# Sink scores and sink AV of a streaming attention as 32-wide tiles of TensorE, with AV banks by head pair

## The chip, the cores and the metric

The kernel runs on one core of a Trainium2 chip. A core has five engines with instruction queues of their own: TensorE (PE in the profile, its weight loads PEld), VectorE (DVE), ScalarE (ACT), GpSimd (POOL) and SyncE (SP). They meet through semaphores. TensorE writes into PSUM, which has eight banks here, and the other engines take the results from there into SBUF. The metric is device time in microseconds (us), the median of several executions.

## What is computed

Sliding-window attention with a few "sink" keys that every query sees, followed by a feed-forward network with the maximum of three products:

```python
batch, n_heads, seq, head_dim = (4, 8, 768, 64)
n_sink, window = (4, 128)
scores = scale * (q @ k.T)
is_sink = pos[None, :] < n_sink
rel = pos[:, None] - pos[None, :]
keep = is_sink | ((rel >= 0) & (rel < window))
a = softmax(where(keep, scores, -1e9))
attn = a @ v                             # heads side by side: x is 3072 x 512
h = maximum(maximum(x @ w1, x @ w2), x @ w3)     # 512 -> 768
out = h @ w_out                          # 768 -> 512
```

Inputs and output are float32; the kernel computes in bfloat16 with float32 sums.

## The kernel before

The 3072 tokens are cut into 12 chunks of 256 queries, three for each of the four batches (`CPB` is 3). A chunk's eight heads are four pairs, one head on partitions 0 to 63, the other on 64 to 127. Chunk number `ci` belongs to batch `ci // 3`; where `ci % 3` is 0 the sink keys lie in the chunk's own window blocks and no separate sink step is needed. The other eight chunks need one.

The order of the work is written out by hand, as strings of short tokens. A token is a step, a letter for a chunk relative to the loop, and an argument. `K`/`Q` transpose keys or queries on TensorE (chunks 0 to 3), `D` has the DMA do it (later chunks) and `E` places the result; `B` and `S` are window scores and their exponentials, `M` the mask, `Z` the sink scores, `X` the copies of sink keys, `A` the product with v, `T` the transpose of x, `F0` to `F8` the nine groups of the first feed-forward layer (number n uses weight n % 3), `Y` and `W` the output layer, `L` the loads. Each engine takes its instructions in this order.

- **Sink keys** (`sink_k`, L235 to L242): for a new batch, four small copies put the four sink keys of each head into a zeroed 128-column stationary matrix `ks` for each pair. For batch 0 ScalarE makes them, for the others VectorE.
- **Sink scores** (`sink_score`, L286 to L296): four matmuls, one per pair, each 128 x 128 stationary and 256 columns, add up into one bank. Row 8x + head of the result is sink key x of that head. One exponential gives `e_sink`.
- **Sink v** (`sink_v`, L171 to L176): the 32 rows of sink v are multiplied by a mask `bm` on GpSimd, so that a row is zero outside its own head's 64 columns, and its last column, where the softmax's sum comes from, is one only there. The result `vs` has 8 x 65 columns for each batch; all of it is zeroed first by ScalarE (L117).
- **AV** (`av`, L300 to L321): a call handles four heads (`g`) and one half of the queries (`t`). In a chunk with sinks it starts with one matmul of `e_sink` against 260 columns of `vs` (L304), then adds eight matmuls of 65 columns (L312). VectorE takes a reciprocal of the sums (L317) and multiplies (L320) into `x_sb`. The calls go in the order g0 t0, g0 t1, g1 t0, g1 t1 in the loop.
- **Transposes of x** (`xpose`, L325): by TensorE and a copy up to chunk 4, later by the DMA from SP's queue. The transpose of half t needs the two calls of `av` that write this half.

All PSUM tiles come from one pool of eight banks with one tag. A tile gets the bank that was given out eight tiles earlier, and its first writer waits until that bank's readers are done.

In the loop over `i`, the letters a, b, c, d, e stand for chunks i to i+4. So TensorE works on the feed-forward of chunk i, on AV of chunk i+1 and the scores of chunk i+2 in one iteration. Before the loop stands a hand-made start in which weights and first chunks arrive. There the loads of weights are issued on GpSimd's queue, among its casts, and some loads are held back by a one-element write of an engine (`load(2, nc.scalar)`): that engine's place in its own queue decides when the load begins.

Of the kernel before, what the change touches and what calls it, by code (L numbers as in the profile page):

```python
# [16 lines left out]
def kernel(  # L17
# [33 lines left out]
    with tc.manual_schedule():  # L51
# [50 lines left out]
        kk = [const.tile([128, NP, 256], BF16, name=f"kk{i}") for i in range(2 * CPB)]  # L102
        qT = [const.tile([128, 2, NP, 128], BF16, name=f"qT{i}") for i in range(2 * CPB)]
        ve = [const.tile([128, S // 128, H, D + 1], BF16, name=f"ve{i}") for i in range(2)]
        ks = [const.tile([128, NP * 130], BF16, name=f"ks{i}") for i in range(2)]
        vs = const.tile([128, B, H, D + 1], BF16, name="vs")

        ident = const.tile([128, 128], BF16, name="ident")
        make_identity(nc, ident)
# [4 lines left out]
            for _ in range(n):  # L114
                nc.tensor.matmul(wp, lhsT=ident, rhs=ident, start=True, stop=True)  # L115

        nc.scalar.copy(vs.rearrange("p b h d -> p (b h d)"), zc.to_broadcast([128, B * H * (D + 1)]))  # L117
        nc.vector.memset(ve[0][:, :, :, D:D + 1], 1.0)
        nc.vector.memset(ks[0], 0.0)

# [39 lines left out]
                    in_=moe_w_out[384 * a:384 * a + 384].rearrange("(a p) f -> p a f", p=128))  # L160


        bm = const.tile([R, H], F32, name="bm")

        def sink_v_init():
            nc.gpsimd.memset(bm, 0.0)
            for x in range(n_sink):
                nc.gpsimd.affine_select(out=bm, in_=bm, compare_op=ALU.not_equal, fill=1.0,
                                        base=-H * x, pattern=[[-1, H]], channel_multiplier=1)

        def sink_v(b):  # L171
            nc.gpsimd.tensor_tensor(
                out=vs[0:R, b, :, 0:D],
                in0=vs_raw[:, b].unsqueeze(1).to_broadcast([R, H, D]),
                in1=bm.unsqueeze(2).to_broadcast([R, H, D]), op=ALU.mult)
            nc.gpsimd.tensor_copy(vs[0:R, b, :, D:D + 1], bm.unsqueeze(2))  # L176

        bfs = {}

# [52 lines left out]
                    out=dst.rearrange("p i a t -> p (i a) t"),  # L232
                    in_=bfs[ci][:, j].rearrange("p i a x -> p (i a x)"))

        def sink_k(b, copy=nc.vector.tensor_copy):  # L235
            kv = ks[b % 2].rearrange("p (a y) -> p a y", y=130)[:, :, 0:8 * n_sink]
            for h in range(2):
                hp = slice(64 * h, 64 * h + 64)
                for i in range(2):
                    copy(  # L240
                        kv[hp].rearrange("p a (t i x) -> p i a t x", i=2, x=8)[:, i, :, :, h],
                        kk[b * CPB % (2 * CPB)][hp, :, 64 * i:64 * i + n_sink // 2])  # L242

        es = {}
# [41 lines left out]
        def sink_score(ci):  # L286
            b, c = divmod(ci, CPB)
            st = psum.tile([128, 256], F32, tag="f", name="sk")
            for p in range(NP):
                nc.tensor.matmul(st, lhsT=ks[b % 2][:, p * 128:(p + 1) * 128],  # L290
                                 rhs=qT[ci % (2 * CPB)][:, :, p].rearrange(
                                     "p i (n t) -> p n i t", n=2),
                                 start=(p == 0), stop=(p == NP - 1))
            e = work.tile([128, 256], BF16, tag="e_sink", bufs=2, name="e_sink")
            nc.scalar.activation(e, st, AF.Exp, scale=scale)  # L295
            es[ci, "sink"] = e  # L296

        xs = {}

        def av(ci, g, t):  # L300
            b, c = divmod(ci, CPB)
            o = psum.tile([128, 4, D + 1], F32, tag="f", name="o_ps")
            if c > 0:
                nc.tensor.matmul(o, lhsT=es[ci, "sink"][:, t * 128:(t + 1) * 128],  # L304
                                 rhs=vs[:, b, 4 * g:4 * g + 4, :], start=True, stop=False,
                                 skip_group_check=True)
            for hh in range(4):
                p, h = divmod(4 * g + hh, 2)
                blocks = [(sl, n) for sl, n in ((2 * t, 2 * c + t - 1), (2 * t + 1, 2 * c + t))
                          if n >= 0]  # L310
                for x, (sl, n) in enumerate(blocks):
                    nc.tensor.matmul(o[:, hh], lhsT=es[ci, p][:, h, sl],  # L312
                                     rhs=ve[b % 2][:, n, 2 * p + h],
                                     start=(c == 0 and x == 0), stop=(x == len(blocks) - 1),
                                     skip_group_check=True)
            rc = work.tile([128, 4], F32, tag="rc", bufs=4, name="rc")
            nc.vector.reciprocal(rc, o[:, :, D])  # L317
            if g == 0:
                xs[ci, t] = work.tile([128, H, D], BF16, tag="x", bufs=4, name="x_sb")
            nc.vector.tensor_mul(xs[ci, t][:, 4 * g:4 * g + 4], o[:, :, 0:D],  # L320
                                 rc.unsqueeze(2).to_broadcast([128, 4, D]))  # L321

        xTs = {}

        def xpose(ci, t):  # L325
            if t == 0:
                xTs[ci] = work.tile([128, 2, DS, 128], BF16, tag="xT", bufs=3, name="xT")
            if ci > CPB + 1:
                nc.sync.dma_start_transpose(
                    out=xTs[ci][:, t], in_=xs.pop((ci, t)).rearrange("p h d -> p (h d)"))  # L330
                return
            pt = psum.tile([128, DS, 128], BF16, tag="f", name="xt_ps")
            x = xs.pop((ci, t)).rearrange("p h d -> p (h d)")
            for ds in range(DS):
                nc.tensor.transpose(pt[:, ds], x[:, ds * 128:(ds + 1) * 128], ident)  # L335
            copy = nc.vector.tensor_copy if ci == 0 else nc.scalar.copy
            copy(xTs[ci][:, t], pt)  # L337
# [57 lines left out]
        def step(op):  # L395
# [6 lines left out]
            elif name == "D":  # L402
                turn(ci)
            elif name == "L":
                load(ci)
            elif name == "E":
                place_k(ci, kTs.pop(ci), slice(0, NP))
            elif name == "S":
                score(ci, [int(x) for x in arg])
            elif name == "B":  # L410
                score_banks(ci, [int(x) for x in arg])
            elif name == "M":
                mask(ci, [int(x) for x in arg])
            elif name == "Z":
                if ci % CPB:
                    sink_score(ci)
            elif name == "X":
                if ci % CPB == 0:
                    sink_k(ci // CPB)
            elif name == "A":  # L420
                av(ci, int(arg[0]), int(arg[1]))
            elif name == "T":
                xpose(ci, int(arg))
            elif name == "F":
                ffn_h(ci, int(arg))
            elif name == "Y":
                ffn_y(ci, [int(arg)], [range(FB)])
            elif name == "W" and ci == NCH - 1:
                ffn_y(ci, [0], [range(FB)])
                ffn_y_end(ci)  # L430
            elif name == "W":
                ffn_y(ci, [0, 1], [range(4), range(4, FB)])

        def run(text, **at):
# [23 lines left out]
        cast_qk(1, 0, 0, nc.vector)  # L458
        cast_qk(1, 1, 0, nc.vector)
        cast_v(0, 1, None, (0,))  # L460
        sink_k(0, nc.scalar.copy)
        cast_qk(1, 0, 1, nc.gpsimd)
        cast_qk(1, 1, 1, nc.gpsimd)
        load_w(1, 0, 256)
        sink_v(0)
        load_w(1, 256, d_ff)
        load_w(2)
        cast_v(1, 0, nc.gpsimd, (0,))
        warm(3)
        run("Aa00 Aa10 Kb0 Qb0", a=0, b=1)  # L470
        run("Aa01 Aa11 Bb01", a=0, b=1)
        run("Sb01 Kb1 Qb1 Ta0 Ta1 Bb23", a=0, b=1)
        run("Sb23 Zb Fa0", a=0, b=1)
        cast_v(1, 0, nc.vector, (1,))
        cast_v(1, 1, nc.vector, (1,))
        cast_v(1, 1, None, (0,))
        run("Fa3 Ab00 Ab10 Ab01 Ab11 Fa6 Tb0 Tb1 Fa1", a=0, b=1)
        load(2, nc.scalar)
        cast_qk(2, 0, 0, nc.gpsimd)
        cast_qk(2, 1, 0, nc.gpsimd)  # L480
        load_wo()
# [2 lines left out]
        load(3, nc.gpsimd)  # L484
        cast_v(2, 0, nc.gpsimd)
        cast_v(2, 1, nc.gpsimd)
        run("Fb0 Fb3 Fb6 Fb1 Fa4 Fa7 Fb4 Fb7 Kc0 Qc0 Fa2 Kc1 Qc1 Fa5 Sc01 Mc01 Fa8 Zc Fb2",
            a=0, b=1, c=2)
        nc.gpsimd.memset(ks[1], 0.0)
        nc.gpsimd.memset(ve[1][:, :, :, D:D + 1], 1.0)  # L490
        cast(3)
        for b in range(1, B):
            sink_v(b)
        load(4)
        run("Fb5 Sc23 Mc23 Ac00 Fb8 Ac01 Ya0 Ya1", a=0, b=1, c=2)
        cast(4)
        run("Ac10 Ac11 Yb0 Tc0 Tc1 Kd0 Qd0 Yb1 Kd1 Qd1", b=1, c=2, d=3)
        run("Zd Sd0123 Md0123 De Lf", d=3, e=4, f=5)

        for i in range(2, NCH):  # L500
# [1 line left out]
                cast(i + 3)  # L502
            text = "Fa0 Fa1 {} Fa2 {} Zc Sc0123 Mc0123 Wa0"
            if i == 2:
                text = text.format("", "Ab00 Fa3 Ab01 Xb Fa4 Ab10 Fa5 Ab11 Fa6 Dd Le Fa7 Fa8 Ya0 Ec Tb0 Tb1 Ya1")
                text = text.replace(" Wa0", "")
            elif i == CPB:
                text = text.format("Ec", "Fa3 Ab00 Fa4 Ab01 Fa5 Ab10 Fa6 Ab11 Dd Le Fa7 Fa8 Tb0 Tb1")
            elif i < 0:
                text = text.format("Ec", "Ab00 Fa3 Xb Ab01 Fa4 Ab10 Fa5 Ab11 Fa6 Dd Le Fa7 Tb0 Tb1 Fa8")  # L510
            else:
                text = text.format("Ec", "Ab00 Fa3 Xb Ab01 Fa4 Ab10 Fa5 Ab11 Tb0 Tb1 Fa6 Dd Le Fa7 Fa8")
            run(text, a=i, b=i + 1, c=i + 2, d=i + 3, e=i + 4)

        for pool in (psum, work, raw, const):
# [36 lines left out]
```

## Time and profile before

| | |
|---|---|
| median of 5 runs | 185.48 us (184.14 to 186.94) |
| the profiled execution | 185.48 us |
| its span in the profile | 183.8 us |
| TensorE busy, matmuls | 172.8 us (94%) |
| TensorE weight loads | 136.6 us (74%) |
| VectorE busy | 119.6 us (65%) |
| ScalarE busy | 91.7 us (50%) |
| GpSimd busy | 71.1 us (39%) |
| granted TensorE clock | 0.994 |

The span runs from the first to the last instruction in the trace; the device time has a little around it. "Busy" of TensorE counts each matmul from start to modelled end, and neighbouring matmuls overlap in a pipeline, so a matmul's own duration is much longer than the step from one to the next. The chain that ended last is followed backwards from the last instruction; in it, a group of matmuls stands with the time by which it moved the end. A group of instructions has the form "line, engine, operation, output<-input, shape, count | busy us, mean ns of one | idle time just before, and what ended it". In a timeline the two leading numbers are start and length in us.

### The profile page before, as it was taken

Reading aid. Unit: us, or ns where it says so; the run is one execution under the profiler, and the core shown is the slowest. Engines: PE = TensorE matmul, PEld = TensorE weight load, DVE = VectorE, ACT = ScalarE, POOL = GpSimd, SP = SyncE. Lnnn points to the kernel's source line nnn. Section 1 sums busy time; section 2 is a strip of 40 time slices with the busy share of each in tenths; the row PEclk is TensorE's granted clock in tenths of the full one; section 3 lists DMA queues with packets and bytes.
Section 4 is the critical chain, followed back from the end, with each engine's and each line's share of the span. In section 5 each row is a group of like instructions: output and inputs, shape, how many; then the busy total and the mean of one; then the engine's idle time right before and its main releaser. Section 6 shows DMA issues by size and latency. Waiting matters only on the chain.

```text
span 183.8 us, 4636 instructions
## 1 busy us (share of the span) xinstructions
PE 172.8 (94%) x1836; PEld 136.6 (74%) x1849; DVE 119.6 (65%) x257; ACT 91.7 (50%) x186; POOL 71.1 (39%) x122
## 2 busy tenths in 40 slices
PE   6987999999997899999999999999999999999990
PEld 6744889876685589589598698697796796896870
DVE  2594626787499189577669686686596775672450
ACT  6398461654941781961832923914716626622210
POOL 7394107748993665392044227145054000000000
PEclk9999999999999999999999999999999999999997
DMA  4999989999878989893698799895996742131404
GB/s 143 296 213 242 213 191 262 208 285 295 253 166 257 203 242 262 229 248 82 145 254 235 158 299 218 224 292 138 146 360 144 92 103 44 43 103 29 116 0 114
DMA packets 68022, 34.67 MB, mean 189 GB/s; under 512 B 26145, under 2 KB 64801, under 8 KB 68001
## 3 DMA queue, kind: packets, MB, share of 16 engines
q1 hardware_dynamic: 64784, 30.45, 65.3%
q0 software_dynamic: 3056, 3.67, 11.4%
q8 instruction: 14, 0.23, 0.5%
q10 hardware_dynamic: 160, 0.26, 0.4%
q14 instruction: 8, 0.06, 0.1%
HBM read 25.20 MB, written 6.29 MB: 171 GB/s over the span
## 4 chain that ended last, share of the span: by engine, by line
PE 79%; DMA 8%; DVE 4%; ACT 2%; issue 1%; POOL 1%; SPq 1%; ACTq 0%; DVEq 0%
PE h_ps L350 48%; PE y_ps L370 16%; DMA v_raw<-in_v_dram 8%; PE o_ps L312 5%; PE st L271 4%; DVE h_sb L356 3%; PE o_ps L304 2%; PE sk L290 2%; SPq L70 1%; POOL ve L197 1%; PE xt_ps L335 1%; PE pt L218 1%; ACT xT L337 1%; DVE x_sb L320 1%; POOL w L150 0%
## 5 line engine op out<-in xcount | busy, mean ns | idle before, releaser
L350 PE MATMUL h_ps<-xT,w 128*128 128x256 bf16 x864 | 103.1, 273 | 1.3 <-DMA w<-in_moe_w_dram 1.2
L350 PEld LDWEIGHTS <-w 128*128 128x128 bf16 x864 | 81.5, 98 | 12.7 <-DMA w<-in_moe_w_dram 1.5
L356 DVE TENSOR_TENSOR h_sb<-h_sb,h_ps 128x512 bf16<-128x512 bf16 x72 | 49.1, 684 | 25.9 <-PE h_ps L350 20.5
L277 ACT ACTIVATE e_sb<-st 128x512 bf16<-128x512 f32 (+1 forms) x96 | 45.1, 591 | 6.9 <-PE st L271 6.9
L188 POOL CAST qk_bf<-qk_raw 128x512 bf16<-128x512 f32 x42 | 28.8, 698 | 50.7 <-DMA qk_raw<-in_k_dram 38.0
L354 ACT CAST h_sb<-h_ps 128x512 bf16<-128x512 f32 x36 | 21.8, 611 | 49.5 <-PE h_ps L350 49.5
L284 DVE TENSOR_TENSOR e_sb<-e_sb,msk 128x1024 bf16<-128x1024 bf16 (+1 forms) x40 | 29.3, 739 | 19.1 <-ACT e_sb L277 19.0
L370 PE MATMUL y_ps<-wo,h_sb 128*128 128x512 bf16 x126 | 31.7, 379 | 2.3 <-DVE h_sb L356 1.6
L197 POOL CAST ve<-v_raw 64x512 bf16<-64x512 f32 x42 | 26.8, 638 | 17.0 <-DMA v_raw<-in_v_dram 13.5
L370 PEld LDWEIGHTS <-h_sb 128*128 128x128 bf16 x138 | 12.8, 98 | 16.2 <-DVE h_sb L356 2.8
L320 DVE TENSOR_TENSOR x_sb<-o_ps,rc 128x256 bf16<-128x256 f32 x48 | 20.4, 424 | 1.6
L312 PE MATMUL o_ps<-ve,e_sb 128*128 128x65 bf16 x352 | 19.0, 193 | 0.9 <-ACT e_sb L277 0.5
L312 PEld LDWEIGHTS <-e_sb 128*128 128x128 bf16 x352 | 17.0, 98 | 2.7 <-ACT e_sb L277 1.1
L380 ACT COPY y_sb<-y_ps 128x512 f32<-128x512 f32 x22 | 12.6, 633 | 11.0 <-PE y_ps L370 10.9
L271 PE MATMUL st<-qT,kk 64*128 64x128 bf16 (+1 forms) x256 | 13.2, 237 | 0.5 <-ACT qT L221 0.3
L271 PEld LDWEIGHTS <-kk 64*128 64x128 bf16 x256 | 8.8, 94 | 5.0 <-issue 3.8
L304 PE MATMUL o_ps<-vs,e_sink 128*128 128x260 bf16 x32 | 8.8, 274 | 0.0
L317 DVE RECIPROCAL rc<-o_ps 128x4 f32<-128x4 f32 x48 | 8.4, 175 | 0.4 <-PE o_ps L312 0.2
L221 ACT COPY qT<-pt 128x512 bf16<-128x512 bf16 x6 | 3.6, 592 | 7.7 <-PE pt L218 7.7
L115 PE MATMUL warm<-ident 128*128 128x128 bf16 x43 | 5.0, 307 | 1.4 <-POOL ident masks.py:199 1.4
L295 ACT ACTIVATE e_sink<-sk 128x256 bf16<-128x256 f32 x8 | 3.2, 394 | 6.4 <-PE sk L290 6.4
L208 DVE COPY kk<-pt 128x512 bf16<-128x512 bf16 x8 | 3.4, 421 | 4.1 <-PE pt L218 4.1
(52 smaller groups left out, 82.5 us busy)
## 6 DMA issues: line engine op xcount, KB each, us to landing
qk_raw<-in_k_dram SPq DMA_DIRECT2D x24, 256.0 KB, 4.1
qk_raw<-in_q_dram SPq DMA_DIRECT2D x24, 256.0 KB, 3.6
v_raw<-in_v_dram SPq DMA_DIRECT2D x11, 512.0 KB, 5.9
out_dram<-y_sb SPq DMA_DIRECT2D x22, 256.0 KB, 4.4
w<-in_moe_w_dram POOLq DMA_DIRECT2D x2, 768.0 KB, 10.8
wo<-in_moe_w_out_dram POOLq DMA_DIRECT2D x2, 384.0 KB, 7.3
v_raw<-in_v_dram POOLq DMA_DIRECT2D x1, 512.0 KB, 9.8
w<-in_moe_w_dram POOLq DMA_DIRECT2D x1, 512.0 KB, 9.3
```

Of the source, the lines that this page charges most:

```text
L188: (eng.tensor_copy if eng else nc.scalar.copy)(dst.rearrange("p i (h d) -> p h i d", d=D), src)
L197: (eng.tensor_copy if eng else nc.scalar.copy)(dst[64 * i:64 * i + 64], src[64 * n:64 * n + 64, :, i])
L271: nc.tensor.matmul(st[h][:, sl], lhsT=kx[r, p, k0:k0 + 128], rhs=qx[r], start=ci >= 2, stop=True, skip_group_check=ci < 2)
L277: nc.scalar.activation(e[:, h, lo:], st[:, lo:], AF.Exp, scale=scale)
L284: nc.vector.tensor_tensor(out=e, in0=e, in1=m, op=ALU.mult)
L312: nc.tensor.matmul(o[:, hh], lhsT=es[ci, p][:, h, sl], rhs=ve[b % 2][:, n, 2 * p + h], start=(c == 0 and x == 0), stop=(x == len(blocks) - 1),
L320: nc.vector.tensor_mul(xs[ci, t][:, 4 * g:4 * g + 4], o[:, :, 0:D], rc.unsqueeze(2).to_broadcast([128, 4, D]))
L350: nc.tensor.matmul(hp[:, f], lhsT=w_sb[wi, 2 * fp + f][:, ds], rhs=xTs[ci][:, :, ds], start=(ds == 0), stop=(ds == DS - 1))
L354: nc.scalar.copy(dst, hp)
L356: nc.vector.tensor_max(dst, dst, hp)
L370: nc.tensor.matmul(yps[ci, t], lhsT=hs[ci][:, fb, t * 128:(t + 1) * 128], rhs=wo[:, fb], start=(fb == 0), stop=(fb == FB - 1))
L380: nc.scalar.copy(y[:, t], yps.pop((ci, t)))
```

## The change

Both sink products become four independent tiles of the array.

- **Sink scores**: a pair's sink keys take a 32-column stationary matrix (8 columns used), and its result goes to 32 partitions of its own, 32p and on, of the one bank. Each matmul is a sum of its own. Row 32p + 2x + h is sink key x of head h in pair p.
- **Sink v**: a selection matrix `sel` is made on GpSimd from the identity. Two matmuls, one for each h, spread the 32 rows of sink v with a column of ones to those partitions for all four batches at once; VectorE copies them to `vs`. ScalarE casts the 32 rows first (into `v_sink`). The mask, its products on GpSimd (one per batch) and the zeroing of `vs` by ScalarE go.
- **Sink AV** is a step of its own, `V`, ahead of the chunk's first `A`. It takes four banks, one for each pair, and issues four matmuls of 32 rows and 130 columns for each half of the queries, each into another bank.
- **AV** goes by pair instead of by four heads and a half: a bank holds both halves of the queries for two heads. Both transposes of x now need all four calls.
- **Sink keys** are copied by ScalarE for all batches.
- **Order**: in the start, `Fa6` moves ahead of chunk 1's AV, the gate of `load(2)` stands right behind that AV, and `Fa4`, `Fa7` come earlier, around the transposes of x. The three late `sink_v` calls on GpSimd go.

```diff
-        ks = [const.tile([128, NP * 130], BF16, name=f"ks{i}") for i in range(2)]
-        vs = const.tile([128, B, H, D + 1], BF16, name="vs")
+        ks = [const.tile([128, NP, 32], BF16, name=f"ks{i}") for i in range(2)]
+        vs = const.tile([128, B, 2, D + 1], BF16, name="vs")
...
-        nc.scalar.copy(vs.rearrange("p b h d -> p (b h d)"), zc.to_broadcast([128, B * H * (D + 1)]))
...
+        def sink_v_init():
+            nc.gpsimd.memset(sel, 0.0)
+            nc.gpsimd.memset(v_sink[:, :, D:D + 1], 1.0)
+            idv = ident[0:R, 0:R].rearrange("r (s p h) -> r p s h", p=NP, h=2)
+            for h in range(2):
+                nc.gpsimd.tensor_copy(sel[:, h, :, 0:2 * n_sink].rearrange(
+                    "r p (s h) -> r p s h", h=2)[:, :, :, h], idv[:, :, :, h])
+
+        def sink_v():
+            for h in range(2):
+                pv = psum.tile([128, B, D + 1], F32, tag="f", name="vs_ps")
+                nc.tensor.matmul(pv, lhsT=sel[:, h].rearrange("r p x -> r (p x)"), rhs=v_sink,
+                                 start=True, stop=True)
+                nc.vector.tensor_copy(vs[:, :, h], pv)
...
-                    copy(
-                        kv[hp].rearrange("p a (t i x) -> p i a t x", i=2, x=8)[:, i, :, :, h],
+                    nc.scalar.copy(
+                        kv[hp].rearrange("p a (t i h) -> p i a t h", i=2, h=2)[:, i, :, :, h],
...
-                nc.tensor.matmul(st, lhsT=ks[b % 2][:, p * 128:(p + 1) * 128],
+                nc.tensor.matmul(st[32 * p:32 * p + 32], lhsT=ks[b % 2][:, p],
                                  rhs=qT[ci % (2 * CPB)][:, :, p].rearrange(
                                      "p i (n t) -> p n i t", n=2),
-                                 start=(p == 0), stop=(p == NP - 1))
+                                 start=True, stop=True)
...
+        def sink_av(ci):
+
+            b = ci // CPB
+            for p in range(NP):
+                ops[ci, p] = psum.tile([128, 2, 2, D + 1], F32, tag="f", name="o_ps")
+            for t in range(2):
+                for p in range(NP):
+                    r = slice(32 * p, 32 * p + 32)
+                    nc.tensor.matmul(ops[ci, p][:, t], lhsT=es[ci, "sink"][r, t * 128:(t + 1) * 128],
+                                     rhs=vs[r, b], start=(t == 0), stop=False,
+                                     skip_group_check=True)
+
+        def av(ci, p):
+
             b, c = divmod(ci, CPB)
-            o = psum.tile([128, 4, D + 1], F32, tag="f", name="o_ps")
...
+            o = ops.pop((ci, p)) if c > 0 else psum.tile([128, 2, 2, D + 1], F32, tag="f", name="o_ps")
+            for t in range(2):
...
+                for h in range(2):
+                    for x, (sl, n) in enumerate(blocks):
+                        nc.tensor.matmul(o[:, t, h], lhsT=es[ci, p][:, h, sl],
+                                         rhs=ve[b % 2][:, n, 2 * p + h],
...
+            rc = work.tile([128, 2, 2], F32, tag="rc", bufs=4, name="rc")
+            nc.vector.reciprocal(rc, o[:, :, :, D])
...
-        run("Fa3 Ab00 Ab10 Ab01 Ab11 Fa6 Tb0 Tb1 Fa1", a=0, b=1)
+        run("Fa3 Fa6 Vb Ab0 Ab1 Ab2 Ab3", a=0, b=1)
         load(2, nc.scalar)
+        run("Fa1 Fa4 Tb0 Tb1 Fa7", a=0, b=1)
...
-        run("Fb5 Sc23 Mc23 Ac00 Fb8 Ac01 Ya0 Ya1", a=0, b=1, c=2)
+        run("Fb5 Sc23 Mc23 Vc Ac0 Fb8 Ac1 Ya0 Ya1", a=0, b=1, c=2)
         cast(4)
-        run("Ac10 Ac11 Yb0 Tc0 Tc1 Kd0 Qd0 Yb1 Kd1 Qd1", b=1, c=2, d=3)
+        run("Ac2 Ac3 Yb0 Tc0 Tc1 Kd0 Qd0 Yb1 Kd1 Qd1", b=1, c=2, d=3)
...
-                text = text.format("Ec", "Ab00 Fa3 Xb Ab01 Fa4 Ab10 Fa5 Ab11 Tb0 Tb1 Fa6 Dd Le Fa7 Fa8")
+                text = text.format("Ec", "Vb Ab0 Fa3 Xb Ab1 Fa4 Ab2 Fa5 Ab3 Tb0 Tb1 Fa6 Dd Le Fa7 Fa8")
```

In the start, `sink_v()` is called once, right behind chunk 1's `Zb Fa0`, and `nc.scalar.copy(v_sink[:, :, 0:D], vs_raw)` stands ahead of the first `sink_k(0)`.

## The prediction

> **What bounds the kernel now.** I read the page first: the span, the chain that ended last, and the groups of the lines that the diff touches.
>
> ```profile
> span 183.8 us, 4636 instructions
> PE 79%; DMA 8%; DVE 4%; ACT 2%; issue 1%; POOL 1%; SPq 1%; ACTq 0%; DVEq 0%
> ...
> L304 PE MATMUL o_ps<-vs,e_sink 128*128 128x260 bf16 x32 | 8.8, 274 | 0.0
> ...
> L290 PE MATMUL sk<-qT,ks 128*128 128x256 bf16 x32 | 4.8, 273 | 0.0
> ```
>
> TensorE carries the chain. A matmul's 273 ns contains latency; back to back the chain gives a sink AV matmul 0.11 us, and four sink scores 0.44. So the two steps hold TensorE for 32 x 0.108 + 8 x 0.44 = 7.0 us, and any gain must come from there, or from the few places where TensorE waits. Next I read the timeline of a steady stretch (chunk 8's scores, iteration 6), start and length:
>
> ```profile
> 99.86 0.60 PE L290 MATMUL sk<-qT,ks 128*128 128x256 bf16 x4
> 100.40 1.06 PE L271 MATMUL st<-qT,kk 64*128 64x128 bf16 x24
> 101.47 2.75 PE L370 MATMUL y_ps<-wo,h_sb 128*128 128x512 bf16 x11
> ```
>
> The scores are already two 64-row tiles at once. Four sink matmuls at 0.109 end at 100.30, yet the scores start at 100.40: entering tile mode costs 0.10. Scores to y take 1.07 for 24 tile matmuls. Streaming them in pairs needs 0.43 x 2 = 0.85 (by columns, against 0.109 per 256), so small tiles with leaving the mode cost 0.22 more.
>
> **Sink scores.** Removed per chunk: 0.44. Added: four column tiles. The row of the score tiles gives about 0.04 us per small tile (1.07 / 24 = 0.045, with the exit), so 0.16, plus 0.10 to enter; the switch into the scores was paid before. 0.44 - 0.26 = about 0.17 saved. The Trainium skill (TensorE: Matmul & The Clock Gate, Part 3) measured three column tiles at 2.38 times, which would give about 0.14 for four, an estimate near my 0.16; but it also says that a weight load overlaps a running matmul only where the row groups differ, and these four share all rows. By that rule they go in turn: 0.44 + 0.10, a loss of 0.10. No column tile is in this trace. I take 0.16 saved, and keep -0.10 to +0.20.
>
> **Sink AV.** Removed per chunk: 4 x 0.109 = 0.44. Added: eight 32-row matmuls of 130 columns. Full overlap would be 2 x 0.054 = 0.11, in turn 8 x 0.054 = 0.43; the 65-column AV matmuls run at 0.24 / 8 = 0.03 and the score tiles at 0.04, so I take 8 x 0.03 = 0.24. Here the skill speaks against the change: TensorEngine Tiling (Array Packing), Key Properties, says that changing the mode, not just the tile, drains TensorE. The trace prices that at 0.10 to enter and up to 0.10 to leave, and this block stands between two full-array steps, so it pays both: 0.44, nothing gained. Without the rule I would book +0.20. I take 0, and keep -0.20 to +0.15. The later AV steps have as many matmuls, reciprocals and multiplies as before, in other shapes: 0.
>
> **One wait is added**, and it is the place I trust most. All four AV banks are now taken before the first pair. Banks go round by eight (in iteration 4 the last scores wait for VectorE's running max in h, which fits). For chunk 2 the fourth bank is that of Fb5, released by the third of these:
>
> ```profile
> 37.68 1.88 DVE L356 TENSOR_TENSOR h_sb<-h_sb,h_ps 128x512 bf16<-128x512 bf16 x3
> 38.19 0.39 PEld L271 LDWEIGHTS <-kk 64*128 64x128 bf16 x12 [0.21 <-issue]
> ...
> 38.74 0.28 PE L304 MATMUL o_ps<-vs,e_sink 128*128 128x260 bf16 x1
> ```
>
> VectorE is done at 39.56; before, this bank went to y at 40.33 without a wait. TensorE would come at 38.74 - 0.17 + 0.2 = 38.8 and stand until 39.6, with Ac0, Fb8, Ac1 and both y groups queued behind it. The saving of this chunk's sink scores is eaten too: -0.75 (-1.0 to -0.3). It reaches the scores of chunk 3, since TensorE has no other gap on the way. Elsewhere the banks are free in time: in iterations 4, 6, 7, 9, 10 the latest is y's, copied by ScalarE about 1.4 us before; in iteration 3 it is the last exponential, which ends at 67.40 against 67.51: 0 to 0.1.
>
> **Sink keys to ScalarE.** In iteration 2 VectorE is the bound:
>
> ```profile
> 55.84 0.52 DVE L240 COPY ks<-kk 64x8 bf16<-64x8 bf16 x4
> ...
> 60.21 0.61 PE L370 MATMUL y_ps<-wo,h_sb 128*128 128x512 bf16 x2 [1.33 <-DVE h_sb L356]
> ```
>
> From the masks at 49.19 VectorE runs without a real gap to 60.16, and y waits. The four copies go: +0.55 (0.3 to 0.55). On ScalarE four such copies took 0.66 at the start; behind them waits Fa6's copy, which had idled 2.65 before its turn. In iterations 5 and 8 TensorE did not wait: 0.
>
> **Transposes come later.** Both need all four pairs now, where the first needed three of the four steps. Iteration 3:
>
> ```profile
> 73.09 0.42 DVE L320 TENSOR_TENSOR x_sb<-o_ps,rc 128x256 bf16<-128x256 f32 x1
> 73.18 0.54 PEld L335 LDWEIGHTS <-x_sb 128*128 128x128 bf16 x8
> ```
>
> The last multiply ends at 73.51, so they start 0.25 later, on a VectorE queue without gaps since 64.49: -0.25, and the sink-score savings of iterations 2 and 3 are lost in this wait and in the exponentials that follow. From iteration 4 on, SP's DMA issues the transposes:
>
> ```profile
> 163.50 3.24 SPq L329 DMA_TRANSPOSE xT<-x_sb  x2
> ...
> 168.72 8.02 PE L350 MATMUL h_ps<-xT,w 128*128 128x256 bf16 x72
> ```
>
> In iteration 10 the last multiply ends at 164.59. Two issues of 1.215 with 2.5 to land, the second from 165.9, land at 168.4 (3.2, the longest, gives 169.1); needed at 168.7: -0.1 (-0.4 to 0). In the other iterations scores stand between, and the transposes, loads and stores behind these on SP's queue move by about 1.1: kT of chunk 7 landed near 90.7 and was used at 93.9, so 0.
>
> **The start.** TensorE begins Fa0 when the first weight, w1, lands:
>
> ```profile
> 18.50 1.92 PE L350 MATMUL h_ps<-xT,w 128*128 128x256 bf16 x16 [1.22 <-DMA w<-in_moe_w_dram]
> ...
> 20.81 0.37 PE L312 MATMUL o_ps<-ve,e_sb 128*128 128x65 bf16 x7 [0.24 <-POOL ve L197]
> ```
>
> Before, Fb0 starts at 24.76 with Fa0, 3, 6, 1 done, and Kc0 eight groups later at 31.74. After: Fa0 to 19.37; the two selection matmuls 2 x 0.108 + 0.2 of switching to 19.8; Fa3, Fa6 to 21.5; sink AV to 22.0; four pairs x 0.24 to 22.95; Fa1, Fa4 to 24.7; transposes to 25.15; Fa7 to 26.0; ScalarE's two copies (1.08) to 26.15; six groups to Kc0 at 31.4. That is +0.35: the waits for v casts and for x are filled by Fa6 and Fa4. VectorE has two more copies of about 0.42 (nearest row: its 256-column copy of y) ahead of two casts of 0.58, done at 21.75, before pair 0 needs block 3. Fa4 needs the second part of w2, issued at 14.34 and landing 9.3 later at 23.6, against 23.8: no margin, so -0.3 to +0.5. The landings follow the bytes queued, so issuing it 1.2 earlier on POOL moves it little.
>
> The rest costs nothing under cover. ScalarE's zero copy (1.92) ends before a 2.76 idle. POOL builds the selection matrix instead of the mask (about 1 us each) ahead of a 2.55 wait for v. The cast of the sink rows (0.39, as e_sink) delays chunk 1's scores by 0.4, hidden by the 1.2 wait for w1; uncovered it would cost 0.4. The gate of load 2 comes some 2.5 us earlier on ScalarE, and POOL loses three sink-v steps (3.4 us at 45.83 to 49.30), so casts and loads come earlier. TensorE waits for none of them; traffic against the weights is unseen, -0.3 to +0.3.
>
> **Sum.** Start +0.35; chunk 2 -0.75; keys +0.55; iteration 3 -0.25; sink scores of iterations 5, 6, 8, 9: 4 x 0.16 = +0.64 (-0.4 to +0.8); sink AV of six iterations 0 (-1.2 to +0.9); iteration 10 -0.1. Together 0.44 us faster. The span is 183.8 and the profiled execution 185.48, 1.7 around it, which stays; that execution is also the median of the five. 185.48 - 0.44 = 185.0.
>
> **Rivals.** (a) Tiles overlap fully: AV +0.15 x 6 and scores +0.20 x 4, chunk 2's wait at its short end (-0.3): 0.35 - 0.3 + 0.55 - 0.2 + 0.8 + 0.9 = 2.1, so 183.4; with the neighbouring VectorE and SP waits easing too, 183. For it: score pairs at 0.107 per two in the 256-column form. Against: the 0.22 lost in the mixed form. (b) Slower: tiles take turns and the drains come on top. AV 8 x 0.054 + 0.2 = 0.63 (-0.20 x 6), sink scores 0.54 (-0.26 x 4 against my sum): 2.2 worse than mine, 187.2. It decides from about 0.23 per block on ten blocks. For it: the overlap rule, and that full-array weight loads hide ahead today while these cannot. Against: row tiles overlap here already. (c) The moved loads and DMA transposes come late: w2's part -0.6, iteration 10 -0.4, chunk 2 -1.0, 186.2. That the tiles aren't taken as tiles at all is (b) without its drains: only my 0.64 is lost, 185.7.
>
> **Numbers.** Mine 0.50 (own range 184.0 to 186.2), (a) 0.25, (b) 0.17, (c) 0.08. Faster by over 1% 0.25, within 1% 0.57, slower 0.18; 1% is about what a measurement of this kernel can tell from no change. Range 182.9 to 187.2.
>
> **What would show it.** The four sink scores some 0.26 from the last full matmul to the scores; sink AV 0.4 per chunk with idle weight loads on both sides; TensorE waiting about 0.8 for VectorE ahead of chunk 2's AV; y of iteration 2 waiting 0.5 less; Kc0 near 31.4. I am wrong if a sink-AV block takes under 0.3 or over 0.6, or if chunk 2's wait is missing.

## The result and the profile after

The changed kernel takes 183.64 us (median of 43 runs) against 184.88 us of the kernel before in the same series (80 runs). The ratio is 0.994, with a 95% interval of 0.9923 to 0.9957: 0.6%, or about 1.1 us, faster. The ratios here leave out executions more than 1.5% above the fastest of their kernel, which the medians include. The profiled execution took 184.03 us, its span is 182.3 us. The forecast was 0.44 us faster and "within 1%". The direction and the band hold, but the gain is two and a half times the forecast, and the sum behind it has errors of both signs. These are what the runs were used for.

The page of the changed kernel, span and chain by engine:

```profile
span 182.3 us, 4683 instructions
...
PE 75%; ACT 7%; DVE 5%; DMA 5%; SPq 3%; issue 3%; ACTq 0%; DVEq 0%
```

TensorE's part of the chain fell from 79% to 75%. The two chains take different paths through the start, so the shares are a rough guide only. But ScalarE, VectorE and SP's queue took over some of it, so part of what TensorE saved went into waits. The table by stage below says where.

The same steady stretch as in the prediction, now with both tile blocks. (It lies in iteration 5 and holds the scores of chunk 7; the prediction calls it iteration 6 and chunk 8.) TensorE's timeline of the changed kernel, start and length; L293 is the sink scores, L313 the sink AV:

```profile
97.81 0.60 PE L364 MATMUL h_ps<-xT,w 128*128 128x256 bf16 x4
98.34 0.29 PE L293 MATMUL sk<-qT,ks 128*32 128x256 bf16 x4
98.56 1.06 PE L274 MATMUL st<-qT,kk 64*128 64x128 bf16 x24
...
102.29 2.78 PE L364 MATMUL h_ps<-xT,w 128*128 128x256 bf16 x24
105.00 0.29 PE L313 MATMUL o_ps<-vs,e_sink 32*128 32x130 bf16 x8
105.23 0.42 PE L326 MATMUL o_ps<-ve,e_sb 128*128 128x65 bf16 x8
105.48 1.03 PE L364 MATMUL h_ps<-xT,w 128*128 128x256 bf16 x8
```

And the weight loads of the two blocks:

```profile
98.34 0.10 PEld L293 LDWEIGHTS <-ks 128*32 128x32 bf16 x4 [0.21 <-issue]
...
105.00 0.12 PEld L313 LDWEIGHTS <-e_sink 32*128 32x128 bf16 x8 [0.21 <-issue]
```

Read by starts: four full matmuls from 97.81 at 0.109 end at 98.25, so entering tile mode costs 0.09. The sink scores then take 0.22 to the start of the window scores. From 98.25 that is 0.31, against 0.54 before (99.86 to 100.40): 0.23 saved. Sink AV comes 0.09 after the last full matmul (102.29 + 24 x 0.109 = 104.91) and takes 0.23, of which 2 x 0.054 = 0.11 are streaming. With the entry that is about 0.32, against 0.44: 0.12 saved. The weight loads of all four tiles lie within 0.10 us, those of all eight within 0.12.

A table by stage says where the time went. The marks are starts on TensorE: Fa0 of the start, Kc0 (transposes of chunk 2), the first scores of chunk 3, and then Fa0 of iterations as the chain gives them. The lengths in us, from one profile of each kernel:

| stage | predicted gain | before | after | gain |
|---|---|---|---|---|
| Fa0 to Kc0 | 0.35 | 13.24 | 12.89 | 0.35 |
| Kc0 to chunk 3's scores (chunk 2's sink AV) | -0.75 | 15.91 | 16.14 | -0.23 |
| chunk 3's scores to iteration 3 (iteration 2) | 0.55 | 16.37 | 14.77 | 1.60 |
| iteration 3 | -0.25 | 14.34 | 14.23 | 0.11 |
| iterations 4, 5, 6 | 0.32 | 39.33 | 38.73 | 0.60 |
| iteration 7 | 0 | 13.07 | 13.93 | -0.86 |
| iterations 8, 9 | 0.32 | 26.26 | 25.93 | 0.33 |
| iteration 10 | -0.1 | 11.86 | 11.75 | 0.11 |

Fa0 itself began 0.33 later (18.83 against 18.50), because the first weight landed later (18.79 against 18.46). ScalarE's exponential of the sink scores ends at 18.79 too, and the profile names that one; but in other profiles of the same start the wait ends with the weight (landed 18.26, Fa0 at 18.30 in the run `vc_later`). The twelve profiles of changed kernels have Fa0 between 17.64 and 19.43, so this belongs to the execution. The stages add up to 2.0 us gained; the later start and the end take 0.5 of it, and the spans differ by 1.5. Three lines need a cause: iteration 2 gained 1.0 more than its copies are worth, chunk 2 lost less, and iteration 7 lost 0.9 that the sum did not have.

### The profile page after: what moved, and what is told of

The parts are those of the page before. It is cut to its first block, busy times and chain, and to the rows that moved or that the text cites. A ratio compares the mean times of both kernels' runs of the same rounds, so it can differ in the third digit from the quotient of the medians.

```text
span 182.3 us, 4683 instructions
## 1 busy us (share of the span) xinstructions
PE 169.5 (93%) x1870; PEld 130.2 (71%) x1883; DVE 116.9 (64%) x247; ACT 92.0 (50%) x198; POOL 67.4 (37%) x113
## 4 chain that ended last, share of the span: by engine, by line
PE 75%; ACT 7%; DVE 5%; DMA 5%; SPq 3%; issue 3%; ACTq 0%; DVEq 0%
PE h_ps L364 45%; PE y_ps L384 15%; PE o_ps L326 6%; ACT e_sb L280 5%; DVE h_sb L370 3%; PE st L274 3%; DMA xT<-x_sb 3%; DMA vs_raw<-in_v_dram 2%; PE pt L221 1%; SPq L97 1%; PE o_ps L313 1%; PE xt_ps L349 1%; SPq L70 1%; PE st L256 1%; PE sk L293 1%
## 5 line engine op out<-in xcount | busy, mean ns | idle before, releaser
L191 POOL CAST qk_bf<-qk_raw 128x512 bf16<-128x512 f32 x42 | 27.3, 655 | 54.2 <-DMA qk_raw<-in_k_dram 46.9
L200 POOL CAST ve<-v_raw 64x512 bf16<-64x512 f32 x42 | 29.7, 708 | 18.5 <-DMA v_raw<-in_v_dram 15.8
L326 PE MATMUL o_ps<-ve,e_sb 128*128 128x65 bf16 x352 | 17.8, 193 | 1.5 <-ACT ve L200 1.1
L326 PEld LDWEIGHTS <-e_sb 128*128 128x128 bf16 x352 | 15.8, 97 | 3.4 <-issue 1.3
L351 ACT COPY xT<-xt_ps 128x512 bf16<-128x512 bf16 x8 | 4.3, 593 | 4.1 <-PE xt_ps L349 4.1
L191 DVE CAST qk_bf<-qk_raw 128x512 bf16<-128x512 f32 x6 | 3.6, 606 | 4.0 <-DMA qk_raw<-in_k_dram 3.3
L221 PE MATMUL pt<-ident,qk_bf 128*128 128x128 bf16 x64 | 5.4, 220 | 0.4 <-DVE qk_bf L191 0.2
```

What stands on the lines that cost most here:

```text
L191: (eng.tensor_copy if eng else nc.scalar.copy)(dst.rearrange("p i (h d) -> p h i d", d=D), src)
L200: (eng.tensor_copy if eng else nc.scalar.copy)(dst[64 * i:64 * i + 64], src[64 * n:64 * n + 64, :, i])
L326: nc.tensor.matmul(o[:, t, h], lhsT=es[ci, p][:, h, sl], rhs=ve[b % 2][:, n, 2 * p + h], start=(c == 0 and x == 0), stop=(x == len(blocks) ...
```

## Experiments

In all of them "the kernel before" is the kernel before the change, run beside them; the ratios are to it.

### GpSimd against VectorE's masks

In iteration 2 the four masks of chunk 3 took 4.24 us before. VectorE's and GpSimd's timelines before:

```profile
49.22 2.92 POOL L188 CAST qk_bf<-qk_raw 128x512 bf16<-128x512 f32 x4
...
49.19 4.24 DVE L284 TENSOR_TENSOR e_sb<-e_sb,msk 128x768 bf16<-128x768 bf16 x4 [1.24 <-ACT e_sb L277]
```

and after:

```profile
46.61 2.28 POOL L191 CAST qk_bf<-qk_raw 128x512 bf16<-128x512 f32 x4
...
49.41 0.56 DVE L287 TENSOR_TENSOR e_sb<-e_sb,msk 128x768 bf16<-128x768 bf16 x1 [1.23 <-ACT e_sb L280]
50.17 2.44 DVE L287 TENSOR_TENSOR e_sb<-e_sb,msk 128x768 bf16<-128x768 bf16 x3 [0.21 <-ACT e_sb L280]
```

The same four masks end 3.20 after they begin. The shortest is 0.56 now and was 0.96 before. The casts of q and k, which used to lie over the first masks, are done before them, since the three sink-v products (3.4 us) left GpSimd's queue; the casts of v lie there now. So GpSimd, which nobody waits for, may have set VectorE's pace. The first run puts products of that size back, into a tile that nobody reads:

```diff
         cast(3)
+        for b in range(1, B):
+            m = vs_raw[:, b, 0:H].unsqueeze(2)
+            nc.gpsimd.tensor_tensor(
+                out=vd[:, b, :, 0:D], in0=vs_raw[:, b].unsqueeze(1).to_broadcast([R, H, D]),
+                in1=m.to_broadcast([R, H, D]), op=ALU.mult)
+            nc.gpsimd.tensor_copy(vd[:, b, :, D:D + 1], m)
         load(4)
```

> The changed kernel, with three products of the old kind (32x512 and a small copy, about 1.24 us each) put back on GpSimd behind the casts of chunk 3, into a tile that nobody reads. Theory (GpSimd's later start moves its q and k casts onto VectorE's masks of chunk 3, and these two slow each other): the four masks of chunk 3 take about 4.2 us again where the changed kernel has 3.2, iteration 2 ends about 1.0 us later, and the whole is about 1.0 us slower than the changed kernel, that is equal to the kernel before. Rival (the shorter masks come from something else): masks stay at 3.2 us and the time stays within 0.3 us of the changed kernel.

Its casts and masks:

```profile
49.79 2.92 POOL L192 CAST qk_bf<-qk_raw 128x512 bf16<-128x512 f32 x4
...
48.59 4.54 DVE L288 TENSOR_TENSOR e_sb<-e_sb,msk 128x768 bf16<-128x768 bf16 x4 [1.24 <-ACT e_sb L281]
```

The masks are back at 4.54, chunk 3's scores to iteration 3 takes 16.10 (14.77 in the changed kernel), and the ratio is 0.9986 (0.9938 to 1.0034) against 0.994; in the time alone the two can't be told apart. The reverse, on the kernel before:

```diff
         cast(3)
-        for b in range(1, B):
-            sink_v(b)
         load(4)
```

> The kernel before, without the three late sink_v calls on GpSimd; sink v of batches 1 to 3 stays zero, so these batches leave out their sinks in the sum and the product. Theory (GpSimd's work against VectorE's masks): the four masks of chunk 3 fall from 4.2 to about 3.2 us, and the kernel gains about 1.0 us (0.5%) although GpSimd is never waited for. Rival: no gain, under 0.3 us.

Masks of 2.86 us, that stage 15.00 instead of 16.37, ratio 0.9912 (0.9831 to 0.9993). The granted clock was low early in its profile (0.54 to 0.61 between 20 and 24 us); in this stage it was 1.00. In the stage both directions agree, 1.33 us lost and 1.37 gained: more than 1 us of iteration 2 comes from taking work off an engine that is idle 60% of the time. Its size varies with the moment at which the casts begin. In the eleven other profiles without the three products the masks took 2.85 to 3.62 us and the stage 14.56 to 15.17.

What a mask takes alone is seen where the casts of v come late, in the run `t_pairs` below:

```profile
48.47 0.56 DVE L287 TENSOR_TENSOR e_sb<-e_sb,msk 128x768 bf16<-128x768 bf16 x1 [1.23 <-ACT e_sb L280]
49.24 0.56 DVE L287 TENSOR_TENSOR e_sb<-e_sb,msk 128x768 bf16<-128x768 bf16 x1 [0.21 <-ACT e_sb L280]
...
50.17 3.08 POOL L200 CAST ve<-v_raw 64x512 bf16<-64x512 f32 x4 [1.86 <-DMA v_raw<-in_v_dram]
```

Beside GpSimd's casts masks took 0.56 to 1.64, and the casts were stretched in their turn. In the kernel before, two casts of 0.60 ran while the first mask took 1.60; behind that, casts took 0.93 and masks 0.96. The Trainium skill names a cause as a rule (GPSIMD Engine Reference, Specifications): GpSimd shares its SBUF interfaces with VectorE, and instructions of VectorE with two SBUF inputs are among those that contend. The masks are of that kind; that it is these interfaces, and no other way for the two to disturb each other, no run here shows.

### The sink keys

```diff
-        def sink_k(b):
+        def sink_k(b, copy=nc.vector.tensor_copy):
...
-                    nc.scalar.copy(
+                    copy(
...
-        sink_k(0)
+        sink_k(0, nc.scalar.copy)
```

> The changed kernel, with the sink keys of batches 1 to 3 copied by VectorE as before. Theory: iteration 2 is bound by VectorE, so the 0.55 us of four copies come back there and y waits that much longer; iterations 5 and 8 unchanged; 0.55 us slower than the changed kernel, 0.5 faster than before. Rival (in the new order VectorE is no longer the bound there): under 0.2 us.

Ratio 0.9942 (0.9898 to 0.9987): no difference from the changed kernel that this many runs can show. In the trace VectorE needs 6.80 us from the first running maximum to the last of iteration 2, where the changed kernel needs 6.23: the 0.57 is on the queue. But the stage is only 0.20 longer (14.97), for in this profile the masks took 2.85, 0.35 less than in the changed kernel's. So the term was right on VectorE, and in the stage it is no larger than the spread that GpSimd gives to the masks.

### Chunk 2's sink AV

Chunk 2's sink AV in the changed kernel stands in the middle of the block, its weight loads too:

```profile
38.61 0.86 PE L313 MATMUL o_ps<-vs,e_sink 32*128 32x130 bf16 x8
39.40 0.42 PE L326 MATMUL o_ps<-ve,e_sb 128*128 128x65 bf16 x8
...
38.60 0.10 PEld L313 LDWEIGHTS <-e_sink 32*128 32x128 bf16 x3 [0.16 <-issue]
...
38.98 0.31 PEld L313 LDWEIGHTS <-e_sink 32*128 32x128 bf16 x5 [0.28 <-issue]
```

and in the chain, time of start and by how much the end moved:

```profile
38.98 0.21 PE o_ps L313
39.20 0.27 PE o_ps L313 x5
```

The block takes 0.79 us to the next AV step instead of 0.23, so 0.56 is waiting. Its third matmul waits for VectorE's second maximum, which ends at 38.93, and starts at 38.98. Its fourth waits for ScalarE's first exponential of the scores just ahead, which ends at 39.15, and starts at 39.20. The third maximum, which ends at 39.53, holds nothing up. So the pool does not give banks strictly eight tiles apart, as I had assumed, and the bank that I took for the fourth's was not its. A run with one group of the feed-forward in between:

```diff
-        run("Fb5 Sc23 Mc23 Vc Ac0 Fb8 Ac1 Ya0 Ya1", a=0, b=1, c=2)
+        run("Fb5 Sc23 Mc23 Fb8 Vc Ac0 Ac1 Ya0 Ya1", a=0, b=1, c=2)
```

> The changed kernel, with chunk 2's sink AV behind Fb8 instead of ahead of it, so that its fourth bank is one that the first exponential of the scores frees, not Fb5's maximum. Theory: the weight loads of sink AV no longer stand (0.28 us in the changed kernel), and some 0.3 us are gained. Rival (the time is only handed on to the next wait, the scores of chunk 3 behind ScalarE's copies): under 0.1 us.

Kc0 to chunk 3's scores takes 15.68 instead of 16.14: 0.46 gained there, and 0.23 less than before the change. In the same profile the masks of chunk 3 took 3.62 and their stage 15.17 instead of 14.77, so 0.40 of it was gone again by iteration 3. Ratio 0.987 (0.9816 to 0.9924), some 1.3 us below the changed kernel's 0.994. That is more than the profile accounts for, and the changed kernel did not run in that series: what the edit is worth in time is open.

### The tiles, each undone

Sink scores with full stationaries; each pair's keys lie at its own 32 of 128 columns, so the result lies where it did:

```diff
-                nc.tensor.matmul(st[32 * p:32 * p + 32], lhsT=ks[b % 2][:, p],
+                nc.tensor.matmul(st, lhsT=ks[b % 2][:, p * 128:(p + 1) * 128],
...
-                                 start=True, stop=True)
+                                 start=(p == 0), stop=(p == NP - 1))
```

> The changed kernel, with the sink scores as four full 128x128 matmuls that add up, each pair's keys at its own 32 of 128 columns, so that the result lies where it did. Theory (four column tiles run at once, and the switch into the scores is paid either way): the step grows from 0.22 to 0.44 us on the chain, and where TensorE is the bound (iterations 5, 6, 8, 9) about 0.2 us each come back, 0.5 to 0.9 us in all. Rival (the switch eats it): the same time within 0.2 us.

TensorE around the sink scores of chunk 7 in this run:

```profile
98.05 0.60 PE L293 MATMUL sk<-qT,ks 128*128 128x256 bf16 x4
98.58 1.06 PE L274 MATMUL st<-qT,kk 64*128 64x128 bf16 x24
```

0.53 again to the window scores. Ratio 0.9987 (0.9963 to 1.0011), 0.0047 above the changed kernel: about 0.9 us, at the upper end of the theory and four times the 0.22 that the block grew by.

Sink AV of chunks 2 and later by the whole array, with sink v padded by zeros to 128 rows per pair (ScalarE zeroes the padded copy in the start, GpSimd fills it):

```diff
-                    r = slice(32 * p, 32 * p + 32)
+                    r = slice(32 * p, 32 * p + 32) if ci == 1 else slice(0, 128)
...
-                                     rhs=vs[r, b], start=(t == 0), stop=False,
+                                     rhs=vs[r, b] if ci == 1 else vf[:, b, p], start=(t == 0), stop=False,
```

> The changed kernel, with sink AV of chunks 2 and later as eight full-array matmuls of 130 columns against sink v padded with zeros to 128 rows for each pair (GpSimd makes the padded copy while it would idle). Chunk 1 keeps the tiles. Theory (eight tiles take 0.22 us with entry, and 0.11 more on leaving, since the next weights cannot be loaded ahead): full-array takes 8 x 0.054 = 0.43 us without a switch, so about 0.1 us per chunk come back, 0.5 to 0.7 us in all. Prediction's value (0.44 for the tile block): no difference.

```profile
105.44 0.63 PE L318 MATMUL o_ps<-vf,e_sink 128*128 128x130 bf16 x8
105.91 0.40 PE L331 MATMUL o_ps<-ve,e_sb 128*128 128x65 bf16 x8
```

The eight full-array matmuls take 0.47 without an entry, against 0.32 with it: 0.15 per chunk. Ratio 0.9999 (0.9972 to 1.0027), 0.0059 above the changed kernel. That is 1.1 us in the time, where the blocks account for 0.15 x 7 = 1.05. But the padding may have its share: the masks of chunk 3 took 3.54 here, and their stage 0.34 more than in the changed kernel. So the 0.15 rests on the rows. They refute the value that the prediction took, no difference.

### The order of the start

```diff
-        run("Fa3 Fa6 Vb Ab0 Ab1 Ab2 Ab3", a=0, b=1)
+        run("Fa3 Vb Ab0 Ab1 Ab2 Ab3 Fa6 Tb0 Tb1 Fa1", a=0, b=1)
         load(2, nc.scalar)
-        run("Fa1 Fa4 Tb0 Tb1 Fa7", a=0, b=1)
...
-        run("Fb0 Fb3 Fb6 Fb1 Fb4 Fb7 Kc0 Qc0 Fa2 Kc1 Qc1 Fa5 Sc01 Mc01 Fa8 Zc Fb2",
+        run("Fb0 Fb3 Fb6 Fb1 Fa4 Fa7 Fb4 Fb7 Kc0 Qc0 Fa2 Kc1 Qc1 Fa5 Sc01 Mc01 Fa8 Zc Fb2",
```

> The changed kernel, with the order of the start as before: Fa3, sink AV and AV, Fa6, transposes, Fa1, then the load of chunk 2; Fa4 and Fa7 back between Fb1 and Fb4. Theory: the keys of chunk 2 are transposed about 0.35 us later, relative to the landing of the first weight, and so is all that follows. Rival (the load of chunk 2 that starts 2 us earlier costs what the order gains): under 0.15 us.

Fa0 to Kc0 is 14.13, 1.24 more than in the changed kernel and 0.9 more than before: in the old order the selection matmuls and VectorE's two copies come on top, and AV and the transposes wait for the v casts and for x. Ratio 0.9977 (0.9955 to 1.0), about 0.7 us worse than the changed kernel. The load of chunk 2 moves with the order, and the run does not tell the two apart. So the tiles with the old order would have cost 0.9 in the start; the new order is what makes up for their price there.

### The transposes of x

Iteration 7 of the changed kernel, from SP's and TensorE's timelines:

```profile
123.33 2.52 SPq L343 DMA_TRANSPOSE xT<-x_sb  x2
...
129.52 1.69 PE L364 MATMUL h_ps<-xT,w 128*128 128x256 bf16 x14 [0.97 <-DMA xT<-x_sb]
```

A transpose landed up to 5.1 us after its issue, where 2.5 is the median, and TensorE stood until the second of the two had landed, at 129.38. The same kernel again, for another profile and then timed:

> The changed kernel once more, for a second profile. Theory: the late landing of the first weight (18.83 us) and the late DMA transpose of iteration 7 (4.8 us to land, TensorE waiting 0.97 us) are of that one execution and do not repeat; the tile blocks (0.22 us each) and the masks of chunk 3 (3.2 us) do. Rival: the transpose is late again, since it now starts behind the store of y.

> The changed kernel, timed beside the next three so that they can be compared. Theory: 0.994 of the kernel before, and in iteration 7 the feed-forward of chunk 8 waits for its DMA transposes again, by 0 to 1 us, since loads that were pushed back by about a microsecond share the DMA engines with them.

The blocks repeated, and the masks nearly (3.21 and 3.40, their stage 14.77 and 14.96). Fa0 began at 17.99 and 18.16. Iteration 7 took 12.96 and 13.25; in the first of the two TensorE and its loads waited for transposes in another iteration instead (8: 13.19 against 12.79), up to 0.9 us. So this wait wanders, but it is there: the longest landing was 4.4 and 4.5, against 3.2 before. Ratio of the timed one 0.9949 (0.9906 to 0.9993).

If the cause is that the first transpose now needs all four pairs, a layout by halves of the pairs should remove it: the first transpose then needs pairs 0 and 1 for all queries.

```diff
-                xs[ci] = work.tile([128, 2, H, D], BF16, tag="x", bufs=2, name="x_sb")
-            nc.vector.tensor_mul(xs[ci][:, :, 2 * p:2 * p + 2], o[:, :, :, 0:D],
+                xs[ci] = work.tile([128, 2, 2, H // 2, D], BF16, tag="x", bufs=2, name="x_sb")
+            nc.vector.tensor_mul(xs[ci][:, p // 2, :, 2 * (p % 2):2 * (p % 2) + 2], o[:, :, :, 0:D],
...
-                                     rhs=xTs[ci][:, :, ds], start=(ds == 0), stop=(ds == DS - 1))
+                                     rhs=xTs[ci][:, ds // 2, :, ds % 2], start=(ds == 0), stop=(ds == DS - 1))
```

> The changed kernel, with x and its transpose laid out by halves of the pairs instead of halves of the queries: the first transpose needs the AV of pairs 0 and 1 alone, the second that of all. Theory (the changed kernel's first transpose is 1.1 us late, and with it everything behind on SP's queue): the first DMA transpose of an iteration starts about 2 us earlier, the wait of chunk 8's feed-forward goes, and the late ones of iteration 3 too; 0.5 to 1.0 us faster than the changed kernel. Rival (the late landing is the traffic of loads alone): the transposes still take over 4 us to land in iteration 7, and the time stays within 0.2 us.

```profile
119.51 3.84 SPq L343 DMA_TRANSPOSE xT<-x_sb  x2
...
127.25 2.78 PE L365 MATMUL h_ps<-xT,w 128*128 128x256 bf16 x24
```

The first transpose starts 7.7 us ahead of its use. In the changed kernel it was 5.2 ahead of 128.55, where TensorE began to wait, and before the change 6.4. No TensorE instruction waits for a DMA transpose any more, and iteration 7 takes 12.95. The landings are no shorter (median 2.7, longest 5.5), so the rival is right that they stay slow, and wrong that this sets the time: the head start covers it. What makes them slow is not shown. Ratio 0.9843 (0.979 to 0.9896); the medians of that series are 182.37 against 183.95 of the changed kernel, 1.6 us. That is more than the 0.5 to 1.0 expected, and in the two profiles 0.40 of it lies in the stage of chunk 3's masks (2.97 against 3.40), which the edit does not touch.

### Together

Both edits, and then with 20 matmuls of the identity where TensorE waits for the first weight:

```diff
-        run("Sb23 Zb Fa0", a=0, b=1)
+        run("Sb23 Zb", a=0, b=1)
+        warm(20)
+        run("Fa0", a=0, b=1)
```

> The last one with chunk 2's sink AV behind Fb8 as well. Theory: the two gains add, some 0.45 us below the last one, 0.988 of the kernel before. Rival: chunk 2's gain is handed to the next wait, the same as the last one.

> The last one with 20 matmuls of the identity (about 1.1 us) between chunk 1's scores and Fa0, where TensorE waits for the first weight. Theory (in profiles where that wait was 1.8 us or more the granted clock was about 0.55 in the next 3.4 us and cost 1.6 us): the clock stays at 1.00 behind the wait in the profile, and the median falls by up to 0.5 us, by as much as that happens in its executions. Rival: the extra matmuls only delay Fa0 where the weight lands early, 0 to 0.3 us slower.

With both edits the ratio is 0.9837 (0.9744 to 0.9929), with the extra matmuls 0.9814 (0.976 to 0.9867). Neither differs from the transposes alone, 0.9843, within these intervals. Chunk 2's gain did not add, as far as this many runs can tell. That the extra matmuls hold the clock is not shown either: their profile waited 1.85 us for the weight with the clock at 1.00 behind it, but so did the changed kernel's after 1.97 us.

## Why the prediction was right, and where its sum was not

- **The result and its size.** 185.0 was forecast from 185.48, that is 0.44 us off; 1.1 came. The case was the likeliest one, gains and losses nearly even. The errors are terms of the sum, and they partly cancel: without the wait of iteration 7, which the sum did not have, the profiled gain would have been about 2.3 us. That the total came as near as it did is in part luck.
- **The start, +0.35:** right to the hundredth from Fa0 on (0.22 to 0.35 in six other profiles with this start and the clock at 1.00 from Fa0 on). Fa4 was not held up, by a hair: its weight landed at 24.00, and its turn came 0.06 later.
- **Sink scores, 0.17 saved each:** mis-sized; 0.23. From the last full matmul to the scores it is 0.31 now. The sum implies 0.54 - 0.17 = 0.37 there; the sign that the prediction named, 0.26, forgot the switch into the scores. The lower bound, tiles in turn by the skill's rule that weight loads overlap only between different row groups, did not occur: four loads of tiles with the same rows lie within 0.10. In iterations 5 and 8 the gain was partly handed on to ScalarE, whose first exponential then ended last ahead of y.
- **Sink AV, nothing saved:** mis-sized; 0.12 saved in place, 0.15 against full-array matmuls of the same columns. I booked 0.24 for eight tiles and 0.20 for the drains on both sides. The tiles overlap fully, so they take 0.11; the other 0.21 of the 0.32 is the switching, as booked. The whole is just above the 0.3 that I had named as a sign of being wrong.
- **Chunk 2's wait, -0.75:** the mechanism was right, the places in the queue wrong. The third bank waits for the second maximum and the fourth for ScalarE, 0.56 together instead of 0.8; the stage lost 0.23, and moving the block gave 0.46 there.
- **Sink keys, +0.55 in iteration 2:** right on VectorE (0.57), 0.20 in the stage of the run that puts them back.
- **What iteration 2 gained beyond that, 1.04:** the step that failed is "the rest costs nothing under cover". I priced the three products leaving GpSimd at nothing because TensorE waits for no cast. VectorE's masks, the bound of that very stage, ran beside those casts.
- **Iteration 3, -0.25:** did not occur, 0.11 gained; in the second profile of the changed kernel it is 14.38, 0.04 lost. The copy that places the keys of chunk 5 on VectorE took 0.41 in the first, where it began ahead of a cast of GpSimd, and x was ready in time. In the second it took 0.79 and before the change 0.85, where a cast was already running, and the transposes of x waited 0.14. So half of the term is there when the copy meets a cast, and the first profile was lucky.
- **The later transposes, -0.1 in iteration 10 and 0 elsewhere:** the direction was right, the place wrong. They cost nothing in iteration 10 and 0.9 in iteration 7, or 0.4 in iteration 8 in the second profile. I had let them land in 2.5 to 3.2 us at any time, and there they took 4 to 5.

## What to carry to other kernels

Small tiles that fill the array paid here even in blocks of four and eight, as long as the block stayed together: price one as the streaming of its concurrent groups plus the switching, about 0.2 us in these traces. A change that delays a step on a DMA queue must be priced at the longest landing and not at the median, and moving the dependency (halves of pairs instead of halves of queries) can be worth as much as the change itself. Work on an idle engine is not free when it slows the one that sets the pace.

## What the runs showed of the hardware that was not expected

Where TensorE waited for the first weight, the granted clock sometimes fell afterwards. The stretches of 2 us from 18 us on in the run with the sink keys on VectorE (length, busy time and count, clock, DMA share, GB/s):

```profile
18.00:20.00 2.00, 1.04 (x9) 1.00 1.31 208
20.00:22.00 2.00, 2.00 (x13) 0.62 1.25 207
22.00:24.00 2.00, 2.00 (x18) 0.53 1.18 210
24.00:26.00 2.00, 2.00 (x46) 1.00 1.14 212
```

In TensorE's timeline of the same run Fa3 and Fa6 are the row at 20.26:

```profile
18.96 1.05 PE L364 MATMUL h_ps<-xT,w 128*128 128x256 bf16 x8 [1.78 <-DMA w<-in_moe_w_dram]
...
20.26 3.42 PE L364 MATMUL h_ps<-xT,w 128*128 128x256 bf16 x16
23.62 0.40 PE L313 MATMUL o_ps<-vs,e_sink 32*128 32x130 bf16 x8
```

To the next step they took 3.36 us instead of 1.86 in the changed kernel, and Fa0 to Kc0 14.50 instead of 12.89: about 1.6 us, more than the change is worth. The wait before was 1.78 us; the changed kernel's profile waited 1.97 and kept its clock. In the second profile of the changed kernel the clock fell at another place, to 0.50 between 12 and 14 us, behind a wait of 1.10 that the first profile has too. There TensorE came to Fa0 at 17.99, just behind the landing of the weight (17.82), so that the lower clock delayed Fa0 by less than 0.2. The Trainium skill (TensorE: Matmul & The Clock Gate, Part 1) has the clock fall after at least one idle window of about 3.4 us, and lets the windows run freely. All waits here are shorter than such a window, so the rule as it stands does not give these falls; that they come in some executions and not in others would fit windows that run freely, but their position can't be seen here.
